# A head's output goes to one of two halves of its PSUM bank by turns, and pools are flushed where the whole plan was drained

## The chip, the cores and the metric

The kernel runs on one core of one Trainium2 chip. The metric is the device time of one execution in microseconds (us). Five engines take part: PE (TensorE, matmuls and transposes), DVE (VectorE), ACT (ScalarE), POOL (GpSimd) and SP (SyncE, which issues DMAs).

## What is computed

Causal attention with a decay bias, then a mixture layer with one dense block ("first MoE"), then one with eight experts and balanced gates ("second MoE"). In short:

```python
def _attn_ref(q, k, v, s):                      # 4 batches, 8 heads, S = 576, D = 64
    scores = (1 / sqrt(D)) * q @ k.T
    cum = cumsum(maximum(s, 0), -1)
    scores = where(causal, -1e9, scores + minimum(-(cum[:, None] - cum[None, :]), 0))
    attn = exp(scores - max(scores)); attn = attn / (sum(attn) + 1e-09)
    return attn @ v
def _moe_ref(x, w_in, w_out):                   # 2304 tokens, 512 -> 2048 -> 512
    h = x @ w_in
    return (h * sigmoid(1.702 * h)) @ w_out
def _moe2_ref(x, w_gate, w1, w2):               # 8 experts, 512 -> 1024 -> 512
    P = exp(x @ w_gate - max); 8 rounds: P by its rows' sums, then by its columns' sums
    return sum over e of P[:, e] * (maximum(x @ w1[e], 0) @ w2[e])
```

## The kernel before

**Attention.** Each of the 4 x 8 (batch, head) pairs is worked on in two parts: query blocks 0 and 1 in one unit, and query blocks 2, 3 and 4 in three units. This gives 64 "heads" n, eight in a row for each half of a batch. For a unit, `scores` makes matmuls into a score bank `sp`, from which DVE takes masked sums and their minimum (`sm`, `stats`) and ACT the exponentials; `turn` transposes them (`tp`) and copies them out (`pf`, or `ph` and `pl` from head 14 on); `values` multiplies them with V into the head's output `op`, 65 columns for each query block, whose last column is the softmax sum. When all units of a head are through, `finish` lets DVE read `op`: TENSOR_SCALAR to `stats`, RECIPROCAL, and SCALAR_TENSOR_TENSOR to `xg` (and `xgl` for the last 64 rows where there are three blocks). After eight heads, `xg` is transposed (`xtp`) and split into `xh` and `xl`, the first MoE's tokens.

**The two MoEs.** The first MoE works on blocks of 256 tokens: `mm1` makes `hp` from `xh`, `xl` and a pair of weights (`wih`, `wil`), ACT and DVE make `t`, `gh` and `gl` from it, and `mm2` adds to `acc` with `woh`, `wol`. The weights are converted on the way (`st`, `t`, casts). The last two blocks are worked on together (`wide1`, `wide2`, tile `accw`). The second MoE follows, with the banks A to D.

**What sets the order.** A planner, the class `Sequencer`, gives every operation a planned time. PE's operations are issued as they come; those of DVE, ACT, POOL and SP are held and handed out by planned time (`run`). So all traced operations have line 279, where the planner calls them, and the tiles' names tell them apart. The main loop asks functions named `can_...` for the planned time from which a step may be taken (`never` if it may not) and takes the first that is due: V's scales, the flush of `xg`, `values`, `turn`, `scores`, and only then a step of the first MoE. `settled(name, ap)` is the planned time at which all operations handed out so far on a tile, or on a part of it, are over, and infinity while one is still held; `slot` asks the same for the next buffer of a tag.

**What the change touches.** `values` takes a new `op` tile for each head from a ring of one buffer (tag "O"), which is one PSUM bank. `can_value` refuses a head that is not the next to be finished (`n > n_fin`) and asks for the slot. `first_moe` waits with `begin` until the attention and its converted weights are through, and then calls `drain`, which hands out everything that is held on all engines, before it closes the attention's pools and calls `begin_second` (which prepares the gate's scale: `gmax`, `wgs`). `flush` of a pool, which exists already, hands out only what touches the pool's tiles, with what that waits for.

Of the kernel before, what the change touches and what calls it, by code (L numbers as in the profile page):

```python
# [9 lines left out]
F32 = mybir.dt.float32  # L10
# [310 lines left out]
def kernel(  # L321
# [12 lines left out]
    seq = Sequencer()  # L334
    nc = Core(seq, tc.nc)
    seq.outside |= {x.tensor.name for x in (qk, vP, s, w_in, w_out, wg, w1, w2, out)}
    B, H, D, S = qk.shape[0], qk.shape[1], qk.shape[2] // 2, qk.shape[3] // 2
# [42 lines left out]
    apool = Pool(seq, pa.enter_context(tc.tile_pool(name="apool", bufs=2, side=right, reuse_waits="tile")))  # L380
# [452 lines left out]
    def turn(i):  # L833
# [21 lines left out]
        )  # L855
        live[i] = (ph, pl, blocks, spots)

    def values(i):
        n, u = units[i]
        qb0 = extent(n)[6][0]  # L860
        v3 = v3_of[n]
        ph, pl, blocks, spots = live.pop(i)
        if u[0] == qb0:
            outs[n] = (
                ps_a.tile([128, 3, D + 1], F32, tag="O", name="op"), stats[:, 8 + n % 2 * 3:11 + n % 2 * 3]
            )
        op, den = outs[n]
        for m, (qb, rows, ke, a) in enumerate(blocks):
            mine = [x for x in spots if x[0] == qb]
            o = op[:rows, qb - qb0, :]  # L870
            for w, (_, kb, _, at) in enumerate(mine):
                if n < N_F:
                    nc.tensor.matmul(
                        o, lhsT=ph[:, at:at + rows], rhs=v3[kb], start=(w == 0), stop=(w == len(mine) - 1)
                    )
                    continue
                for part, nv in ((ph, 2), (pl, 1)):
                    for j in range(nv):
                        v = v3[j][:, kb, :]
                        nc.tensor.matmul(  # L880
                            o[:, 0:v.shape[1]], lhsT=part[:, at:at + rows], rhs=v,
                            start=(w == 0 and part is ph and j == 0),
                            stop=(w == len(mine) - 1 and part is pl and j == nv - 1),
                        )
# [81 lines left out]
    def can_value():  # L966
        if n_v >= n_t or units[n_v][0] not in v3_of:
            return never
        n, u = units[n_v]
        if n > n_fin:  # L970
            return never
        x = [live[n_v][0], live[n_v][1], *v3_of[n]]
        return max([seq.slot(ps_a, "O") if n not in outs else 0] + [seq.settled(a.tensor.name) for a in x])

    def do_value():
        nonlocal n_v
# [918 lines left out]
    def first_moe():  # L1895

        at_pair = [0] * NB1

        def can(j):
            p = at_pair[j]  # L1900
            if p == NPAIR or 4 * p + 2 > n_conv:
                return never
            return max(
                whole(j) if at_pair[j] == 0 else 0, seq.slot(ps_m, "h"),
                seq.settled(wih[p].tensor.name), seq.settled(wil[p].tensor.name),
            )

        def second(i):
            def when():
                j, p, gh, gl = pend[0]  # L1910
                if 4 * p + 4 > n_conv:
                    return never
                t = max(seq.settled(x.tensor.name) for x in (gh, gl, woh[p], wol[p]))
                if p == 0 and i == 0:
                    t = max([t] + [
                        seq.slot(*x) for x in
                        ([(ps_a, "S1"), (ps_a, "T1")] if j == 1 else [(ps_m, "acc0"), (ps_m, "acc1")])
                    ])
                return t

            return when

        for item in range((NB1 - 2) * NPAIR):

            js = (0, 1) if item < 2 * NPAIR else (item // NPAIR,)
            yield lambda: min(can(j) for j in js)
            j = min(js, key=can)
            p = at_pair[j]
            at_pair[j] += 1
            if (j, p) == (1, 0):  # L1930
                lent[0] = True
            mm1(j, p, 0)
            yield lambda: 0
            mm1(j, p, 1)
            if at_pair[j] == NPAIR and j + 2 < NB1:
                alloc_x(j + 2)
            for i in range(2):
                if item:
                    yield second(i)
                    mm2(i)  # L1940

        def begin():
            if n_conv < len(chunks) or n_fin < len(heads) or any(pieces.values()) or vpows:
                return never
            return max(whole(j) for j in (NB1 - 2, NB1 - 1))

        for i in range(2):
            yield second(i)
            mm2(i)
        yield begin  # L1950
        seq.drain()
        pa.close()
        begin_second()
        for n in range(2 * NPAIR):
            p, i = NPAIR - 1 - n // 2, n % 2
            wide1(p, i)
            yield lambda: 0
            if n:
                wide2()
                yield lambda: 0  # L1960
            if (p, i) == (NP0 - 1, 0):
                p1b.close()
                begin_weights()
# [297 lines left out]
```

## Time and profile before

| | us |
|---|---|
| time, median of 3 runs | 1994.68 (1994.12 to 1995.38) |
| the profiled execution | 1995.91 |
| its span in the trace | 1994.1 |
| PE busy in the span | 1956.2 (98%) |
| DVE, ACT, POOL busy | 1427.6, 1227.5, 335.0 |
| PE idle in the span | 37.9 |

The profile comes from one execution, recorded by the hardware profiler. The time of an execution is a little longer than its span, which runs from the first to the last recorded instruction. An engine's busy time is a sum over stages with different limits; idle time is found by cutting the span into stretches and by reading an engine's timeline, where each idle stretch stands in square brackets with what ended it. The first part of the span, up to about 545 us, holds the attention with the first MoE's work between its steps; the wide blocks begin at about 573 us.

### The profile page before, as it was taken

How to read it: one execution, taken by the hardware profiler on the slowest of the kernel's cores; microseconds unless marked ns; L12 is line 12 of the kernel's file. 1: busy time of each engine (PE TensorE's matmuls, PEld its weight loads, DVE VectorE, ACT ScalarE, POOL GpSimd, SP SyncE). 2: the span in 40 equal slices, each digit the busy share in tenths (PEclk: the TensorE clock that was granted, in tenths of full speed). 3: DMA queues.
4: the chain of work that ended last, by engine and by line, in shares of the span. 5: the costliest groups of instructions: out<-in, count | busy, mean ns of one | idle time of the engine just before them, and what ended most of it. 6: DMA issues, size and time to landing. Idle time of an engine off the chain costs nothing.

```text
span 1994.1 us, 41095 instructions
## 1 busy us (share of the span) xinstructions
PE 1956.2 (98%) x15683; PEld 1575.5 (79%) x15683; DVE 1427.6 (72%) x3240; ACT 1227.5 (62%) x2525; POOL 335.0 (17%) x376
## 2 busy tenths in 40 slices
PE   6999999999999999999999999999999999999999
PEld 5889999999988677777777777777777777777777
DVE  5886776776743776887877767776787776776656
ACT  4776765766643665665666666656666666565343
POOL 3565444443300000000000011111100001111000
PEclk9999999999999999999999999999999999999999
DMA  7555444454335544565484565666648556566331
GB/s 221 159 178 181 138 131 138 129 146 116 86 94 186 208 152 146 202 232 182 147 273 133 153 186 156 172 197 184 167 120 261 147 150 186 156 172 183 119 130 43
DMA packets 230100, 322.11 MB, mean 162 GB/s; under 512 B 38272, under 2 KB 156224, under 8 KB 229904
## 3 DMA queue, kind: packets, MB, share of 16 engines
q1 hardware_dynamic: 216944, 295.90, 45.2%
q0 software_dynamic: 12960, 23.60, 8.2%
q8 instruction: 123, 2.02, 0.4%
q14 instruction: 73, 0.60, 0.1%
HBM read 230.85 MB, written 84.34 MB: 158 GB/s over the span
## 4 chain that ended last, share of the span: by engine, by line
PE 81%; DVE 9%; ACT 6%; DMA 2%; issue 1%; SPq 0%; POOL 0%; ACTq 0%; DVEq 0%
PE C L279 16%; PE A L279 16%; PE D L279 16%; PE hp L279 8%; PE B L279 8%; PE acc L279 5%; PE op L279 3%; PE sp L279 3%; PE tp L279 2%; ACT h L279 2%; PE accw L279 2%; DVE h L279 2%; DVE t L279 1%; DVE hst L279 1%; PE accx L279 1%
## 5 line engine op out<-in xcount | busy, mean ns | idle before, releaser
L279 PEld LDWEIGHTS <-h 128*128 128x128 f16 x6048 | 591.3, 98 | 86.3 <-issue 7.6
L279 PEld LDWEIGHTS <-w1o 128*128 128x128 f16 x4036 | 394.6, 98 | 255.1 <-issue 4.5
L279 POOL DMA_DIRECT2D acc_d<-y x90 | 77.8, 865 | 1186.5 <-DVE y L279 662.1
L279 PE MATMUL C<-xt,w1o 128*128 128x384 f16 x1152 | 218.6, 326 | 1.4 <-DVE hst L279 1.4
L279 PE MATMUL D<-xt,w1o 128*128 128x384 f16 x1152 | 218.4, 326 | 0.0
L279 PE MATMUL D<-w2o,h 128*128 128x256 f16 x1728 | 217.7, 273 | 0.2 <-ACT y L279 0.2
L279 PE MATMUL A<-xt,w1o 128*128 128x384 f16 x1152 | 214.8, 326 | 0.1
L279 PE MATMUL A<-w2o,h 128*128 128x256 f16 x1728 | 212.2, 273 | 1.7 <-ACT B L279 1.4
L279 PE MATMUL C<-w2o,h 128*128 128x256 f16 x1728 | 208.4, 273 | 2.5 <-DVE y L279 1.7
L279 DVE SCALAR_TENSOR_TENSOR h<-hst,h 128x768 f16<-128x768 f32 (+1 forms) x192 | 139.1, 755 | 55.9 <-ACT h L279 55.9
L279 ACT COPY C<-B 128x384 f32<-128x384 f32 (+1 forms) x168 | 71.5, 426 | 153.8 <-PE B L279 92.7
L279 PE MATMUL hp<-xh,wih 128*128 128x256 f32 (+1 forms) x512 | 154.4, 302 | 1.3 <-DVE t L279 0.7
L279 PE MATMUL hp<-xl,wih 128*128 128x256 f32 (+1 forms) x512 | 152.0, 297 | 0.0
L279 PE MATMUL hp<-xh,wil 128*128 128x256 f32 (+1 forms) x512 | 151.8, 297 | 0.0
L279 ACT ACTIVATE h<-hst 128x768 f16<-128x768 f32 (+1 forms) x192 | 126.2, 678 | 3.8 <-DVE hst L279 3.8
L279 ACT ACTIVATE sm<-sm,stats 64x576 f32<-64x576 f32 (+4 forms) x160 | 94.5, 600 | 34.0 <-DVE stats L279 33.7
L279 PE MATMUL acc<-gh,woh 128*128 128x256 f32 x384 | 110.9, 289 | 0.0
L279 PE MATMUL B<-w2o,h 128*128 128x256 f16 x864 | 110.5, 273 | 0.1
L279 PE MATMUL B<-xt,w1o 128*128 128x384 f16 x576 | 109.3, 326 | 0.0
L279 PE MATMUL acc<-gl,woh 128*128 128x256 f32 x384 | 108.5, 282 | 0.0
L279 PE MATMUL acc<-gh,wol 128*128 128x256 f32 x384 | 108.3, 282 | 0.0
L279 ACT COPY B<-A 128x384 f32<-128x384 f32 (+1 forms) x168 | 70.2, 425 | 58.4 <-PE A L279 57.6
(242 smaller groups left out, 4041.8 us busy)
## 6 DMA issues: line engine op xcount, KB each, us to landing
xt<-xc_d SPq DMA_DIRECT2D x168, 384.0 KB
wm<-in_moe_w_dram SPq DMA_DIRECT2D x112, 256.0 KB
w2o<-w_d SPq DMA_DIRECT2D x56, 512.0 KB
wr<-in_moe_w_dram SPq DMA_DIRECT2D x112, 256.0 KB
w_d<-wo SPq DMA_DIRECT2D x98, 256.0 KB
acc_d<-y POOLq DMA_DIRECT2D x90, 256.0 KB, 4.8
kq<-in_qk_dram SPq DMA_DIRECT2D x32, 448.0 KB
st<-in_moe_w_in_dram SPq DMA_DIRECT2D x16, 512.0 KB
```

The source lines that it names most:

```text
L279: self.seq.submit(self.name, what, lambda: method(*args, **named), outs, ins, "accum_op" in named)
```

## The change

All heads' outputs share one tile, `o_all`, of two halves of three blocks each. Head n uses half n modulo 2. `can_value` lets head n start when head n-1 is not yet finished (`n > n_fin + 1` is refused), and asks the planner for that half only. At the end of the first MoE's blocks, `drain` is replaced by a flush of the two pools that are closed next.

```diff
--- before.py
+++ after.py
@@ -855,15 +855,15 @@
         )
         live[i] = (ph, pl, blocks, spots)
 
+    o_all = ps_a.tile([128, 2, 3, D + 1], F32, name="op")
+
     def values(i):
         n, u = units[i]
         qb0 = extent(n)[6][0]
         v3 = v3_of[n]
         ph, pl, blocks, spots = live.pop(i)
         if u[0] == qb0:
-            outs[n] = (
-                ps_a.tile([128, 3, D + 1], F32, tag="O", name="op"), stats[:, 8 + n % 2 * 3:11 + n % 2 * 3]
-            )
+            outs[n] = o_all[:, n % 2], stats[:, 8 + n % 2 * 3:11 + n % 2 * 3]
         op, den = outs[n]
         for m, (qb, rows, ke, a) in enumerate(blocks):
             mine = [x for x in spots if x[0] == qb]
@@ -967,10 +967,10 @@
         if n_v >= n_t or units[n_v][0] not in v3_of:
             return never
         n, u = units[n_v]
-        if n > n_fin:
+        if n > n_fin + 1:
             return never
         x = [live[n_v][0], live[n_v][1], *v3_of[n]]
-        return max([seq.slot(ps_a, "O") if n not in outs else 0] + [seq.settled(a.tensor.name) for a in x])
+        return max([seq.settled(o_all.tensor.name, o_all[:, n % 2]) if n not in outs else 0] + [seq.settled(a.tensor.name) for a in x])
 
     def do_value():
         nonlocal n_v
@@ -1948,7 +1948,8 @@
             yield second(i)
             mm2(i)
         yield begin
-        seq.drain()
+        apool.flush()
+        ps_a.flush()
         pa.close()
         begin_second()
         for n in range(2 * NPAIR):
```

Three places of the built program follow. Names carry a buffer number; [waits X] are the engines (or DMA queues) on whose progress the instruction waits, DVE_49 being DVE's and PE_49 PE's.

PE, the second head's output at the start of the attention. Before:

```order
L279 MATMUL tp_320<-ident_60,sm_263 128x128 [waits PE_49,Activation_49]
L279 MATMUL tp_320<-ident_60,sm_263 128x128 [waits Activation_49]
L279 MATMUL tp_320<-ident_60,sm_263 128x128
L279 MATMUL sp_340<-kf_239 128x128 [waits DMAHW1_49,DMAHW0_49,DVE_49]
L279 MATMUL sp_340<-kf_239 128x256
L279 MATMUL sp_346<-kf_249 128x128 [waits DMAHW3_49,DMAHW2_49,DVE_49]
L279 MATMUL sp_346<-kf_249 128x256
L279 MATMUL op_366<-vf0_133,pf_298 128x65 [waits DVE_49,PE_49]
L279 MATMUL op_366<-vf0_133,pf_298 128x65
L279 MATMUL op_366<-vf1_134,pf_298 128x65
```

After:

```order
L279 MATMUL tp_320<-ident_60,sm_264 128x128 [waits PE_49,Activation_49]
L279 MATMUL tp_320<-ident_60,sm_264 128x128 [waits Activation_49]
L279 MATMUL tp_320<-ident_60,sm_264 128x128
L279 MATMUL op_141<-vf0_133,pf_299 128x65 [waits DVE_49]
L279 MATMUL op_141<-vf0_133,pf_299 128x65
L279 MATMUL op_141<-vf1_134,pf_299 128x65
L279 MATMUL tp_337<-ident_60,sm_284 128x128 [waits PE_49,Activation_49]
L279 MATMUL tp_337<-ident_60,sm_284 128x128 [waits Activation_49]
L279 MATMUL tp_337<-ident_60,sm_284 128x128
L279 MATMUL sp_349<-kf_240 128x128 [waits DMAHW1_49,DMAHW0_49]
L279 MATMUL sp_349<-kf_240 128x256
```

The second head's `op` (its `pf` is number 298 before, 299 after) has moved ahead of four `sp` and waits for DVE alone.

DVE ahead of the first `hp`. Before, `two1` and the rows behind it, and further on the two first `xl`:

```order
L279 TENSOR_TENSOR two1_115<-kq_359,one1_114 64x576
L279 SCALAR_TENSOR_TENSOR xg_308<-op_487,stats_124 128x2x64 [waits DVE_49]
L279 SCALAR_TENSOR_TENSOR t64_261<-st_247 128x512 [waits DMAHW4_49,Activation_49,Pool_49]
L279 TENSOR_SCALAR stats_124<-op_515 128x2 [waits PE_49]
L279 CAST wih1_76<-t64_261 128x512 [waits DVE_49]
L279 RECIPROCAL stats_124<-stats_124 128x2 [waits DVE_49]
L279 SCALAR_TENSOR_TENSOR t64_268<-st_255 128x512 [waits DMAHW3_49,Activation_49,Pool_49]
L279 SCALAR_TENSOR_TENSOR xg_308<-op_515,stats_124 128x2x64 [waits DVE_49]
L279 ISA sm_524,stats_124<-sp_525,mask_120 128x384 [waits PE_49]
```

```order
L279 TENSOR_TENSOR xl_128<-xtp_582,xh_127 128x4x128 [waits Activation_49]
L279 CAST one0_112<-kq_360 128x896 [waits DMAHW5_49,DMAHW2_49]
L279 SCALAR_TENSOR_TENSOR t64_280<-st_258 128x512 [waits DMAHW4_49,Pool_49]
L279 COPY pf_621<-tp_615 128x320 [waits DVE_49,PE_49]
L279 TENSOR_TENSOR xl_128<-xtp_601,xh_127 128x4x128 [waits Activation_49]
```

After:

```order
L279 SCALAR_TENSOR_TENSOR xg_308<-op_141,stats_124 128x2x64 [waits DVE_49]
L279 TENSOR_TENSOR two1_115<-kq_370,one1_114 64x576 [waits DMAHW7_49,Activation_49]
L279 CAST woh0_74<-t64_257 128x512 [waits DVE_49]
L279 SCALAR_TENSOR_TENSOR t64_260<-st_238 128x512 [waits DMAHW1_49,Pool_49]
L279 TENSOR_TENSOR xl_128<-xtp_504,xh_127 128x4x128 [waits Activation_49]
L279 CAST woh0_74<-t64_260 128x512 [waits DVE_49]
L279 SCALAR_TENSOR_TENSOR t64_262<-st_248 128x512 [waits DMAHW2_49,Activation_49,Pool_49]
L279 TENSOR_TENSOR xl_128<-xtp_510,xh_127 128x4x128 [waits Activation_49]
```

`xg` of the eighth head (the first row after) now stands directly ahead of `two1`, and the two `xl` follow within seven rows, with two `t64` and two `woh` casts between them; before, 24 rows lie between `two1` and the first `xl`.

PE and DVE where two heads of three blocks meet. PE before, at the start of a head's `op`:

```order
L279 MATMUL hp_788<-xh_127,wih1_76 128x256
L279 MATMUL hp_788<-xl_128,wih1_76 128x256
L279 MATMUL hp_788<-xh_127,wil1_77 128x256
L279 MATMUL op_808<-vf0_133,pf_762 128x65 [waits DVE_49,Activation_49]
L279 MATMUL op_808<-vf1_134,pf_762 128x65
L279 MATMUL op_808<-vf2_135,pf_762 128x65
```

PE after:

```order
L279 MATMUL op_141<-vf3_136,pf_775 64x65
L279 MATMUL op_141<-vf4_137,pf_775 64x65
L279 MATMUL op_141<-vf0_133,pf_786 128x65 [waits DVE_49,Activation_49]
L279 MATMUL op_141<-vf1_134,pf_786 128x65
L279 MATMUL op_141<-vf2_135,pf_786 128x65
```

DVE before, the division of such a head:

```order
L279 TENSOR_SCALAR stats_124<-op_697 128x2 [waits PE_49]
L279 TENSOR_TENSOR wil2_81<-t64_386,wih2_80 128x512 [waits Activation_49]
L279 TENSOR_SCALAR stats_124<-op_697 64x1
L279 SCALAR_TENSOR_TENSOR t64_420<-st_279 128x512 [waits DMAHW3_49,Pool_49]
L279 SCALAR_TENSOR_TENSOR t_742<-t_742,hp_670 128x512 [waits Activation_49]
L279 RECIPROCAL stats_124<-stats_124 128x3 [waits DVE_49]
L279 COPY pf_768<-tp_763 128x512 [waits PE_49]
L279 SCALAR_TENSOR_TENSOR xg_645<-op_697,stats_124 128x2x64 [waits DVE_49]
L279 SCALAR_TENSOR_TENSOR xgl_646<-op_697,stats_124 64x64
```

DVE after:

```order
L279 TENSOR_SCALAR stats_124<-op_141 128x2 [waits PE_49]
L279 TENSOR_TENSOR wil2_81<-t64_427,wih2_80 128x512 [waits Activation_49]
L279 TENSOR_SCALAR stats_124<-op_141 64x1 [waits PE_49]
L279 SCALAR_TENSOR_TENSOR t64_463<-st_280 128x512 [waits DMAHW4_49,Pool_49]
L279 RECIPROCAL stats_124<-stats_124 128x3 [waits DVE_49]
L279 ISA sm_777,stats_124<-sp_827,mask_120,stats_124 64x288 [waits PE_49]
L279 ISA stats_124 64x1
L279 SCALAR_TENSOR_TENSOR xg_669<-op_141,stats_124 128x2x64 [waits DVE_49,PE_49]
L279 SCALAR_TENSOR_TENSOR xgl_670<-op_141,stats_124 64x64
```

On PE the next head's `op` (`pf_786`) follows the last one's (`pf_775`) with nothing between them and waits for DVE, where `hp` matmuls stood ahead of it; on DVE the first `xg` now waits for PE as well as for DVE's own reciprocal.

## Rows read from the trace of the kernel before

**Rows 1.** The page's busy times (share, instructions), and the chain that ended last.

```profile
PE 1956.2 (98%) x15683; PEld 1575.5 (79%) x15683; DVE 1427.6 (72%) x3240; ACT 1227.5 (62%) x2525; POOL 335.0 (17%) x376
...
PE 81%; DVE 9%; ACT 6%; DMA 2%; issue 1%; SPq 0%; POOL 0%; ACTq 0%; DVEq 0%
```

**Rows 2.** Stretches of 100 us: length, busy us (count) by engine, PEclk, DMA share, GB/s.

```profile
0.00:100.00 100.00, 82.03 (x533) 72.14 (x533) 72.45 (x222) 61.83 (x111) 45.30 (x60) 1.00 0.62 190
100.00:200.00 100.00, 94.04 (x858) 89.65 (x858) 77.60 (x190) 70.62 (x142) 58.62 (x54) 0.97 0.56 179
200.00:300.00 100.00, 99.16 (x1014) 94.70 (x1012) 75.14 (x241) 69.64 (x147) 43.82 (x51) 1.00 0.47 135
500.00:600.00 100.00, 98.45 (x801) 89.36 (x802) 60.34 (x182) 51.02 (x105) 19.55 (x21) 1.00 0.34 96
```

**Rows 3.** PE's waits: engine tile <- releaser: us in total, times, longest us.

```profile
PE op L279 <- DVE xg L279: 6.7, 7, 2.4
...
PE op L279 <- DVE xgl L279: 1.6, 2, 0.8
```

**Rows 4.** PE's timeline, 20 to 60 us: start, us, operation, [idle before <- releaser].

```profile
20.38 1.51 PE L279 MATMUL op<-vf,pf 128*128 128x65 f32 x6
...
24.60 1.51 PE L279 MATMUL op<-vf,pf 128*128 128x65 f32 x6 [0.79 <-DVE xg L279]
...
36.24 1.51 PE L279 MATMUL op<-vf,pf 128*128 128x65 f32 x6 [1.13 <-DVE xg L279]
...
41.54 1.52 PE L279 MATMUL op<-vf,pf 128*128 128x65 f32 x6 [2.44 <-DVE xg L279]
...
49.00 0.65 PE L279 MATMUL xtp<-ident,xg 128*128 128x128 f32 x4
49.49 0.78 PE L279 MATMUL op<-vf,pf 128*128 128x65 f32 x6
...
50.39 0.40 PE L279 MATMUL sp<-two 68*128 68x512 f32 x1
...
55.30 0.36 PE L279 MATMUL hp<-xh,wih 128*128 128x256 f32 x1
```

**Rows 5.** DVE's timeline, 21 to 25 us.

```profile
21.93 0.16 DVE L279 TENSOR_SCALAR stats<-op 128x2 f32<-128x2 f32 x1 [0.68 <-PE op L279]
...
22.62 0.16 DVE L279 RECIPROCAL stats<-stats 128x2 f32<-128x2 f32 x1
23.95 0.29 DVE L279 CUSTOM_DVE_ANT_0 sm<-sp,mask 128x128 f32<-128x128 f32 x1 [1.17 <-ACT st L279]
...
24.17 0.28 DVE L279 SCALAR_TENSOR_TENSOR xg<-op,stats 128x128 f32<-128x128 f32 x1
```

**Rows 6.** PE's timeline, 9.5 to 9.9 us: the last matmuls into a score bank.

```profile
9.23 1.06 PE L279 MATMUL sp<-kf 66*128 66x256 f32 x2
```

**Rows 7.** DVE's timeline, 10 to 11 us: its first reading of that bank.

```profile
10.45 0.29 DVE L279 CUSTOM_DVE_ANT_0 sm<-sp,mask 128x128 f32<-128x128 f32 x1 [4.87 <-PE sp L279]
```

**Rows 8.** DVE's groups by shape, 5 to 570 us: busy us, mean ns, idle before.

```profile
L279 DVE SCALAR_TENSOR_TENSOR t<-st 128x512 int32<-128x512 int32 x32 | 30.0, 943 | 1.1 <-POOL wol L279 0.7 <-ACT va L279 0.3
...
L279 DVE TENSOR_TENSOR xl<-xtp,xh 128x512 fp32r<-128x512 f32 x12 | 8.2, 681 | 1.1 <-ACT xh L279 1.1
L279 DVE CAST woh<-t 128x512 fp32r<-128x512 f32 x12 | 7.8, 649 | 0.1
...
L279 DVE TENSOR_TENSOR two<-kq,one 64x576 fp32r<-64x576 f32 x1 | 1.4, 1441 | 0.0
```

**Rows 9.** PE's timeline, at 301 us and at 503 us.

```profile
301.60 0.22 PE L279 MATMUL op<-v,ph 128*128 128x65 f16 x2 [0.41 <-DVE xg L279]
...
503.57 0.22 PE L279 MATMUL op<-v,ph 128*128 128x65 f16 x2 [0.76 <-DVE xgl L279]
```

**Rows 10.** Two shorter stretches; columns as in Rows 2.

```profile
99.80:117.75 17.95, 15.44 (x167) 13.79 (x167) 13.88 (x45) 15.26 (x32) 8.94 (x10) 0.89 0.47 152
110.00:121.00 11.00, 8.49 (x67) 7.28 (x66) 9.88 (x28) 9.82 (x23) 5.93 (x8) 0.69 0.70 235
```

## The prediction

> **What bounds the kernel now.** The page's busy table comes first: PE works 98% of the span, and the chain that ended last is PE for 81% of it [rows 1]. An edit can therefore win only where PE stands idle or runs below full speed. The table by stretches says where that is: PE is busy for 82.03 us of the first 100, 94.04 of the second and 99.16 of the third, at a granted clock of 1.00, 0.97 and 1.00 [rows 2]. So some 24 us are idle in the first 200 us, under 1 us in the next 100, and 1.55 us between 500 and 600 us.
>
> The third view is PE's waits. Those of the `op` matmuls for DVE's reading of the head before (`xg`, `xgl`) are 6.7 + 1.6 = 8.3 us [rows 3]. That is the whole sum at which the first part of the change aims. PE's timeline places it: four waits early on, twice 0.79 or 0.80 (one is shown), 1.13 and 2.44, 5.16 us together [rows 4], and then single ones, of which those of 0.41 and 0.76 are shown [rows 9]. What makes the first wait long is seen on DVE: `op` of one head ends at 21.89 [rows 4], its `stats` starts at 21.93, but `xg` only at 24.17, because DVE handles its list in order and a score reading stands in front of it until 23.95 [rows 5]. 0.15 us after `xg` ends, the next head's `op` starts.
>
> **The change part by part.** In the order as built, PE's instructions are the same in number, and from about 545 us on in the same sequence. So all that can move lies in the first 545 us.
>
> *Two halves for `op`, early heads.* The planner now lets `op` of head n+1 go out before head n is divided, into the other half. But the built program still waits for all that touches the bank, whichever half it is: 54 `op` matmuls carry a wait on DVE's reads (17 before), some 45 of them on the other half, and some 31 DVE reads wait for the other head's matmuls (none before). So a wait leaves its place and comes back in another form. That the program makes bank-wide waits can be seen in this trace too: DVE's reading of the first 128 columns of a score bank starts at 10.45 [rows 7], 0.16 us after the end of the matmuls into that bank's other 256 columns, at 10.29 [rows 6].
>
> The Trainium skill ("PSUM — Partial Sum Buffer", section "PSUM bank collisions raise a hardware error") has a rule on the same side, and against this change: PSUM has to be guarded by bank and quadrant, not by address, since two engines on one bank collide at different columns as well. The row at 10.45 agrees. By the rule both halves stay one resource; without it the whole 8.3 us would be open, which is the third rival below.
>
> Of the four early waits I expect three to come back, smaller. The least that one costs is `stats` alone between two heads: 0.04 + 0.16 + 0.15 = 0.35 us; the most with nothing else on DVE is `stats`, reciprocal and `xg` in a row: 0.04 + 0.16 + 0.16 + 0.28 + 0.15 = 0.79 us, as the waits of 0.79 and 0.80 show. I take 0.72 each, so 2.2 us remain of 5.16 and 3.0 are saved.
>
> What is late next: the first MoE matmul `hp`. It now comes after 78 matmuls instead of 121, and needs `xl` of all its 256 tokens. On DVE there now stand between the last early `xg` and the second `xl` one `two`, two `t`, two `woh` casts and two `xl`: 1.44 + 2 x 0.94 + 2 x 0.65 + 2 x 0.68 = 6.0 us [rows 8], about 5.5 with each starting some 0.07 before the last one's end (23.95 + 0.29 and 24.17 show it [rows 5]). PE has eight `xtp` and four `sp` to do meanwhile: 2 x 0.65 + 4 x 0.40 = 2.9 us as at 49 to 51 us, and up to twice that at the lower speed, at which six `op` took 1.51 us instead of 0.78 [rows 4]. So 0 to 2.6 us of new idle time; I take 1.5, since at 49 us PE ran at full speed. Sum of the early phase: -3.0 + 1.5 = **-1.5 us**, between -5.2 (nothing comes back) and 0 (all comes back).
>
> *New waits on the bank after 50 us.* In the built order there are 13 places where an `op` waits for the other half's reader with at most 0.8 us of PE work since the matmuls that the reader needs; the third order piece shows one with none. Price: the rows nearest to it are the waits of 0.41 and 0.76 us [rows 9]; I take the lower, 0.4 each, since up to 0.8 us of work lies ahead of the waiting matmul. Five of the 13 lie in the stretch of the next term. The other eight cost 8 x 0.4 = 3.2, all 13 5.2 us. The waits of this kind that go with the old order are 8.3 - 5.16 = 3.1 us, of which I credit 2.3: the one of 0.76 at 503.57 has DVE late by its own work, and should stay. So +0.9 to +2.9; I take **+1.9 us**. Bounds: -2.3 (none of the 13 waits) to 13 x 0.76 - 2.3 = +7.6.
>
> *A longer run of attention only.* The order before has two stretches with 60 or more matmuls in a row and none from the MoE, of 121 and 72; after, there are three, of 169, 78 and 61. The run of 72 ends at 117.75 us. It is what such a run costs: 17.95 - 15.44 = 2.5 us idle, at a granted clock of 0.89, with ACT (15.26) and DVE (13.88) as busy as PE; and a clock of 0.69 over 11.00 us, which is 3.4 us of work lost at the lower level (1.2 of 2.4 GHz) if it is all counted [rows 10]. The clock fell while PE was idle between short `op` and `xtp` matmuls. The run of 169 has the same contents, 2.3 times as many. Ends: -3.4 if the fall of the clock does not come back, and (2.5 + 3.4) x 1.35 = +8.0 if the loss grows with the length. The middle is +2.3; I take **+2.0**, a little lower, because the longer run begins nearer to MoE work at full speed.
>
> *Flush instead of drain at 573 us.* PE's order does not change through this part. It moves the small operations for the gate's scale on DVE ahead of the first wide `t` and `gl`, and the gate weights' DMA ahead of the writes of `x_d` on SP. Behind them on DVE waits a `gl`, and for that one PE matmul group; PE's idle time between 500 and 600 us is 1.55 us in all [rows 2], with 0.76 of it at 503.57 [rows 9]. So the gain is at most 0.8, and a loss at most one 512-column operation, 0.68 [rows 8]. **0**, since DVE is busy for 60.34 of these 100 us and has room.
>
> Sum: -1.5 + 1.9 + 2.0 + 0 = **+2.4 us**. The profiled execution took 1995.91, 1.8 us of it outside the span, which nothing touches; it stood 1.23 us above the median of 1994.68. So 1998.3 by that execution, and 1994.68 + 2.4 = **1997.1 us** as a median.
>
> **The rivals.**
>
> *Slower: the long run is paced by DVE and ACT at the lower clock.* Place: the 169 matmuls ahead of 118 us. For it: the shorter run already fell to 0.69, and the new run also has five of the 13 bank waits, whose idle time is what the clock fell after. Against it: the run starts with PE at full speed. It decides from the point where the clock falls in the first half of the run. Then the third term is +8.0: -1.5 + 1.9 + 8.0 = +8.4, 2003.1 us.
>
> *Faster: the early waits go and the clock holds.* `op` of head n+1 waits only for a short `stats`, which DVE has long done; `xl` is ready in time; the fall at 110 to 121 us does not recur. That is -3.0 + 0 + 0.9 - 3.4 = -5.5, and, if early matmuls get to full speed a few us sooner (those of 1.51 against 0.78 us), a further 1 to 2 us: 1988 us. For it: PE's speed rose at about 49 us, after a row of work without a wait. Against it: DVE's list, not only PE's place in it, makes the early waits.
>
> *The change does what it says: the halves are independent.* All 8.3 us go and nothing takes their place: 1986.4 us. Against it stand the waits in the built program, and the row at 10.45.
>
> **How the numbers follow.** Within 0.2% means within about 4 us, 1990.7 to 1998.7, about what a measurement of this kernel can tell from no change. The forecast has 0.47, with its own range of 1992 to 2002: 0.37 of it within 0.2%, and 0.10 above. The slower rival has 0.25, the faster one 0.21, independent halves 0.07. Faster is 0.21 + 0.07 = 0.28, same 0.37, slower 0.10 + 0.25 = 0.35. The range runs from 1987, just under the faster rival, to 2006, which is 3 us over the slower one because its price is scaled from one shorter run; about 0.1 is left out at each end.
>
> **What would show it.** PE's idle time ahead of the early `op` matmuls (5.16 us before) should fall to about 2 us, and ahead of the first `hp` there should be 1 to 2 us of wait for `xl`. The table of PE's waits should show `op` waiting for `stats` as well as `xg`, in more and shorter waits, some 5 us after 50 us. In 60 to 120 us the granted clock should fall at least once, to about 0.7 over 10 us. From 200 us to the end the busy share should stay. If the clock row of that stretch reads 1.00 throughout, or the first `hp` starts 5 us earlier than 55.30 [rows 4] without a later run idling, the forecast is wrong on the faster side; if the clock falls at the start of the long run, on the slower side.

## The result and the profile after

The changed kernel takes **2006.45 us** (median, 2003.58 to 2007.74), the kernel before 1994.76 (1994.12 to 1995.38): a ratio of 1.0057, with an interval of 1.0039 to 1.0074. It is slower, by 11.7 us, where 2.4 us were forecast. In the experiments below, single executions of 3002, 5078 and 7422 us are left out of the ratios. Each ratio is to the kernel before as measured beside it; in the four sets of experiments its median lay between 1993.5 and 1996.1 us, so kernels of different sets are compared by their ratios.

| profiled execution | before | after |
|---|---|---|
| time, us | 1995.91 | 2007.74 |
| span | 1994.1 | 2005.9 |
| PE busy / idle in the span | 1956.2 / 37.9 | 1967.2 / 38.7 |
| start of the first wide block (`accw`) | 573.5 | 585.9 |
| at the lower clock after 52 us | 6.8 | 13.65 |

The last row is worked out from the granted clock of stretches of 5 us: a stretch of 5 us at 0.78, for example, had 2 x (1 - 0.78) x 5 = 2.2 us at the lower level. The page of after, engines and chain of waits, to be held against [rows 1]:

```profile
PE 1967.2 (98%) x15683; PEld 1580.7 (79%) x15683; DVE 1430.3 (71%) x3248; ACT 1223.8 (61%) x2515; POOL 333.6 (17%) x378
PE 79%; DVE 9%; ACT 6%; DMA 2%; issue 1%; SPq 1%; POOL 0%; ACTq 0%; DVEq 0%
```

PE has as many instructions and almost the same idle time; it was *busy* for 11 us more. The rows count a matmul as busy to its modelled end: at full clock an `hp` has 0.28 us, but the next one starts 0.12 us after it. So a successor that is a little late, and the lower clock too, add to the busy time, and the busy share alone hides the loss. By the distances between the starts of PE's rows, from 52 us to the first wide block after needs about 13 us more than before; an estimate from these rows gives 3 to 4 us of it to idle time, 3 to 4 to the lower clock and some 6 to matmuls that follow each other later at full clock. Where the loss lies is told by a landmark. The rows of the first `accw` matmuls (count: least/median/most ns, first and last start), of before and then of after:

```profile
L279 PE MATMUL accw<-gh,woh x64: 388/389/397, 573.5 to 654.8; 128*128 128x512 f32 x64
```

```profile
L279 PE MATMUL accw<-gh,woh x64: 387/389/495, 585.9 to 667.6; 128*128 128x512 f32 x64
```

12.4 us are lost by 586 us, and none behind that. The table by stretches of after (length, then busy time of PE, PEld, DVE, ACT, POOL, granted clock, DMA share, GB/s) answers to [rows 2]:

```profile
0.00:100.00 100.00, 84.70 (x529) 74.29 (x530) 62.31 (x210) 61.83 (x113) 42.99 (x58) 0.98 0.62 189
100.00:200.00 100.00, 90.72 (x819) 83.84 (x817) 81.50 (x194) 71.21 (x141) 60.65 (x60) 0.95 0.52 165
200.00:300.00 100.00, 98.25 (x955) 93.00 (x954) 67.09 (x210) 61.20 (x125) 36.03 (x42) 1.00 0.43 126
500.00:600.00 100.00, 98.60 (x868) 90.22 (x867) 64.56 (x196) 55.51 (x115) 22.63 (x24) 1.00 0.30 80
```

The second hundred has lost 3.3 us of PE's time and some clock, the third 0.9. The clock falls in three places, where before it fell in one. Stretches of 5 us of after:

```profile
75.00:80.00 5.00, 4.21 (x29) 3.66 (x28) 4.24 (x13) 3.65 (x7) 1.89 (x2) 0.88 0.78 242
80.00:85.00 5.00, 5.00 (x38) 4.71 (x38) 2.21 (x11) 3.24 (x6) 1.81 (x3) 0.78 0.50 163
110.00:115.00 5.00, 3.38 (x31) 2.94 (x32) 4.48 (x10) 2.92 (x7) 3.50 (x5) 0.79 0.34 93
115.00:120.00 5.00, 5.00 (x39) 5.00 (x39) 4.37 (x16) 2.86 (x7) 2.36 (x3) 0.86 0.13 30
180.00:185.00 5.00, 3.00 (x31) 1.81 (x27) 5.00 (x11) 3.37 (x7) 2.05 (x3) 0.96 0.71 241
185.00:190.00 5.00, 4.79 (x33) 4.57 (x34) 3.00 (x9) 3.85 (x7) 1.67 (x2) 0.50 0.29 100
190.00:195.00 5.00, 5.00 (x34) 4.57 (x34) 2.60 (x7) 3.66 (x8) 2.60 (x3) 0.86 0.60 184
```

Each fall comes in, or right behind, a stretch in which PE stood idle for 0.8 to 2 us of 5. In the last group the reader sees why PE was idle: DVE is busy for all of the 5 us. The rows of DVE and PE there (start, duration, operation, and in brackets the idle time and what ended it):

```profile
181.27 1.26 DVE L279 SCALAR_TENSOR_TENSOR t<-st 128x512 int32<-128x512 int32 x1
182.46 0.68 DVE L279 SCALAR_TENSOR_TENSOR pl<-tp,ph 128x512 f16<-128x512 f32 x1
...
183.19 0.20 PE L279 MATMUL op<-v,pl 128*128 128x65 f16 x1 [1.36 <-DVE pl L279]
```

`op` waits for `pl`, and `pl` stood on DVE behind `t`, a step of the conversion of weights for the first MoE; DVE has two of these `t` and three operations on what they made (`woh`, `wol`) between 179 and 185 us. Before, PE is busy for all of the stretch of 180 to 195 us, at a clock of 1.00:

```profile
180.00:195.00 15.00, 15.00 (x138) 14.51 (x137) 6.94 (x24) 8.58 (x15) 4.44 (x6) 1.00 0.43 144
```

PE's waits of after (us in total, times, longest):

```profile
PE op L279 <- DVE pl L279: 4.1, 6, 1.4
PE op L279 <- DVE xg L279: 2.4, 4, 1.4
PE hp L279 <- DVE xl L279: 2.0, 1, 2.0
PE op L279 <- DVE stats L279: 1.8, 5, 0.6
...
PE xtp L279 <- DVE pl L279: 1.7, 2, 1.1
PE tp L279 <- ACT sm L279: 1.7, 2, 1.0
PE sp L279 <- DVE stats L279: 1.5, 3, 0.8
```

The wait that the change aims at fell from 8.3 us [rows 3] to 2.4 + 1.8 = 4.2. What rose is waits for other readers and writers on the way of a head: `pl`, `sm`, `xl`. Before, those of `op` for `pl` were

```profile
PE op L279 <- DVE pl L279: 2.6, 4, 1.1
```

So the named waits do not add up to the loss. A second measure does: **the lag**. For a given amount of PE's matmul work (each matmul counted at the usual distance of its shape at full clock), it is the time at which a kernel has done it less the time at which before had. It is worked out from PE's rows, in us, from one profiled execution of each kernel; the columns are before's times. Its accuracy is limited: o_all_drain, told below, has after's PE order and comes to about +6 at 186 us and +10.2 at the first `accw`, so 2 us between two kernels may be a difference of executions, and at 63 us the value moves by about 1 us with the distance that is taken for each shape.

| kernel | 63 | 90 | 118 | 142 | 164 | 186 | 291 | first `accw` |
|---|---|---|---|---|---|---|---|---|
| after | -2.4 | +1.5 | +3.2 | +1.7 | +3.1 | +8.7 | +12.0 | +12.4 |
| after_free | -5.4 | -4.9 | -4.4 | -4.6 | -1.7 | +2.7 | +4.1 | +4.5 |
| new_rule_first_8 | -3.1 | -0.1 | +2.8 | +2.6 | +5.3 | +6.6 | | +7.0 |
| two_banks_first_8 | -4.7 | -0.1 | +2.0 | +2.0 | +4.3 | +5.9 | | +6.8 |
| planner_sees_bank | +0.7 | -0.4 | -0.3 | -1.9 | +5.4 | +4.3 | | +5.5 |
| conversion_first | -0.7 | -0.1 | -0.1 | +0.6 | -0.3 | +2.0 | | +5.6 |
| new_rule_from_9 | +0.8 | -0.7 | +2.5 | -0.2 | +0.2 | +0.7 | | +13.9 |

The lower rows are experiments, told below.

### The profile page after: what moved, and what is told of

Same layout as the page of the kernel before. It is cut to its first block, busy times and chain, and to the rows that moved or that the text cites. A ratio compares the mean times of both kernels' runs of the same rounds, so it can differ in the third digit from the quotient of the medians.

```text
span 2005.9 us, 41081 instructions
## 1 busy us (share of the span) xinstructions
PE 1967.2 (98%) x15683; PEld 1580.7 (79%) x15683; DVE 1430.3 (71%) x3248; ACT 1223.8 (61%) x2515; POOL 333.6 (17%) x378
## 4 chain that ended last, share of the span: by engine, by line
PE 79%; DVE 9%; ACT 6%; DMA 2%; issue 1%; SPq 1%; POOL 0%; ACTq 0%; DVEq 0%
PE C L279 16%; PE A L279 16%; PE D L279 16%; PE B L279 8%; PE hp L279 8%; PE acc L279 5%; PE op L279 3%; PE sp L279 3%; PE tp L279 2%; ACT h L279 2%; PE accw L279 2%; DVE h L279 2%; DVE hst L279 1%; DVE t L279 1%; DVE sa L279 1%
```

## The experiments

The theory after the result: the loss is made by the new order of PE's and DVE's work (the rule in `can_value`), in part through waits on the shared bank, in part through conversions of weights that come late. Rivals: the tile's layout or the flush; the bank alone; the clock alone.

**Which part of the change.** First the halves and the flush with the old rule, so that PE's instructions stand in before's order; then the new rule with the old drain.

```diff
-        if n > n_fin + 1:
+        new = False
+        if n > n_fin + (1 if new else 0):
...
-        return max([seq.settled(o_all.tensor.name, o_all[:, n % 2]) if ...
+        return max([seq.settled(o_all.tensor.name, o_all[:, n % 2] if new else None) if ...
```

> Halves and flush as in the change, but a head may still start only when the one before is divided and the whole bank is free in the plan. PE's order is then that of the kernel before on all its instructions. Theories 'order' and 'bank': 1994.8 us, within 1 us of the kernel before, since no wait for the other half is left in the way. If the tile's new place or the flush is the cause: 2000 us or more.

Measured: 1994.81 us, a ratio of 1.0004 (0.9995 to 1.0014).

```diff
-        apool.flush()
-        ps_a.flush()
+        seq.drain()
```

> The two halves alone; the drain at the end of the first MoE's blocks is kept as before. Its PE order is that of the changed kernel. Both theories put the whole loss into the first 545 us: 2006 us, within 1 us of the changed kernel. A third theory, that the flush costs several us by what it leaves on DVE ahead of the first wide block: 2003 us or less.

Measured: 2005.61 us, 1.0056 (1.0040 to 1.0072). PE's order of tiles in the traces is before's in the first kernel and after's in the second. So the layout and the flush cost and gain nothing that a measurement tells from zero, and the loss belongs to the new rule.

**Which heads.** The rule for the first eight heads alone (`new = n < 8` in the first diff), and from the ninth on (`new = n >= 8`).

> The changed kernel, but the new rule for the start of a head holds for the first 8 heads only; from the ninth on a head starts when the one before is divided and the whole bank is free. Theory 'conversion late': in the changed kernel the attention goes ahead faster from the start, the conversion of the first MoE's weights (handed out with the lowest rank) ends at 181 us instead of 163, and between 170 and 190 us PE has attention alone, with DVE full; the first heads set this off, so this kernel still ends its conversion after 172 us and takes 2000 to 2004 us. Theory 'bank': what counts is the number of waits on the other half, and these are mostly gone here: 1994 to 1998 us.

Measured: 2002.95 us, 1.0044 (1.0030 to 1.0059).

> The opposite piece: the first 8 heads by the old rule, the rest by the new one. 'Conversion late': the start is as before, the conversion ends before 170 us, 1994 to 1999 us. 'Bank': most of the waits on the other half are in this piece, 2001 to 2005 us.

Measured: 2006.66 us, 1.0067 (1.0052 to 1.0082). Each part of the rule costs by itself, and they do not add: about 9 and 13 us, by the ratios, against 11.7 for both. The second result lies nearer to the theory "bank", which had expected 2001 to 2005 us, than to that of late conversions, 1994 to 1999. The rule for the first eight heads loses by 186 us, after a gain of 3.1 us at 63; that for the other heads loses most far later, at 360 us, where the profile of new_rule_from_9 shows

```profile
360.22 0.22 PE L279 MATMUL op<-v,ph 128*128 128x65 f16 x2 [1.98 <-DVE xg L279]
```

and, in that stretch, an idle PE and a fall of the clock, where before had none (the second line is before's):

```profile
355.00:375.00 20.00, 17.66 (x170) 16.18 (x169) 13.70 (x44) 12.11 (x25) 5.20 (x7) 0.83 0.30 88
```

```profile
355.00:375.00 20.00, 20.00 (x236) 18.66 (x235) 15.39 (x48) 16.46 (x32) 9.44 (x11) 1.00 0.55 164
```

This wait is one for the bank, and in all the bank's waits of this kernel are as long as before's:

```profile
PE op L279 <- DVE xg L279: 8.6, 8, 2.4
```

The profiled execution (2009.95 us) was the slowest of four, 3.3 us above their median, so its lag is somewhat high. Still, the loss is not tied to one place of the program: the two parts of the rule lose at different places, each where the new sequence leaves PE waiting.

**What the shared bank costs.** DVE's division of a head reads a constant tile (`ident`) instead of `op`, while the planner still believes that it reads `op`. PE's and DVE's order stays, and no division waits for the bank or holds it.

```diff
-                out=den[:r, c0:c1], in0=op[:r, c0:c1, D], ...
+                    out=den[:r, c0:c1], in0=ident[:r, 0:c1 - c0], ...
-                in0=op[:r, c0:c1, 0:D], ...
+                    in0=ident[:r, 0:(c1 - c0) * D].rearrange("p (a d) -> p a d", a=c1 - c0), ...
```

> The changed kernel in its own order, but DVE's division of a head reads a constant tile in SBUF in place of the output bank, so that no matmul and no division waits for that bank (the attention's result is therefore not the reference's). Theory 'order': the 11.7 us come from the new order, in which PE stands idle for reads of other tiles (pl, sm, xl, xtp) and its clock falls more often; this kernel then stays at 2000 to 2004 us, and 8 us or more above the same edit of the kernel before. Theory 'bank': the waits on the other half of the bank are the loss, with the clock falls that follow them; this kernel then comes to 1993 us or less, and to no more than the same edit of the kernel before.

Measured: 2001.36 us, 1.0038 (1.0024 to 1.0051).

> The kernel before in its own order with the same edit (the division reads a constant tile, so the attention's result is not the reference's). Its op matmuls waited 8.3 us for the division. Both theories: faster than before by at most those 8.3 us and by what the clock gives back, 1986 to 1993 us; if DVE's other work is late at the same places, nearer to 1993. What tells the theories apart is the distance to the other kernel of this kind: 'order' 8 to 12 us, 'bank' 0 us or below.

Measured: 1997.68 us, 1.0016 (1.0006 to 1.0025). That is *slower* than before by 3.3 us, where both theories had expected it to be faster, and the distance of the two edited kernels is 3.7 us, between the 8 to 12 of the theory "order" and the 0 of the theory "bank". In after's order the edit is worth 2005.61 - 2001.36 = 4.3 us against o_all_drain beside it, and 5.1 against after itself.

These are not clean prices of the waits, for the edit also made DVE's division longer. The operation that writes most of `xg` (mean ns after the busy time), before and in before_free:

```profile
L279 DVE SCALAR_TENSOR_TENSOR xg<-op,vpow,stats 128x128 f32<-128x128 f32 x50 | 17.2, 344 | 12.4 <-PE xtp L279 12.0
```

```profile
L218 DVE SCALAR_TENSOR_TENSOR xg<-ident,vpow,stats 128x128 f32<-128x128 f32 x50 | 29.1, 583 | 12.6 <-PE xtp L280 12.2
```

In all DVE is busy for 1454.4 us in before_free against 1427.6 in before, and for 1450.0 in after_free against 1430.3 in after. For the heads behind the eighth, no run takes the waits away without this. If the edit by itself costs after's order the 3.3 us that before lost by it, the bank's share would be 7.5 us instead of 4.3; that is an estimate, and the share of the order alone would then be the 3.7. In after_free, `op` and `tp` wait longer for `pl` and `sm` than in after, which fits a later DVE:

```profile
PE op L280 <- DVE pl L280: 5.0, 6, 1.6
PE tp L280 <- ACT sm L280: 2.8, 4, 0.9
```

The lag says when: without the bank the new order is 5.4 us ahead at 63 us and still 4.6 at 142; with it, 2.4 ahead and then 1.7 behind. From 142 to 186 us both lose about the same, 7.3 and 7.0 us (o_all_drain some 5). So that second loss is there without any wait for the bank, though the longer division may have a part in after_free's.

A real second bank for the odd ones of the first eight heads (a tile of `ps_m`, which is not in use yet) points the same way. PE's and DVE's order is that of new_rule_first_8:

```diff
-    o_all = ps_a.tile([128, 2, 3, D + 1], F32, name="op")
+    def op_bank(n):
+        return (ps_m, "acc1") if n < 8 and n % 2 else (ps_a, "O")
...
```

> The first 8 heads' outputs go by turns to two whole banks (the second is one that the first MoE needs only from about 61 us on); from the ninth head on the old rule and one bank. The order is that of the kernel with the new rule for the first 8 heads (2002.95 us); only the waits on the other half are gone. 'Bank' for these heads: the stretch up to 60 us ends 5 us earlier than in the kernel before (in the changed kernel with no bank waits at all it was 5.4), and the time comes to 1996 to 1999 us. 'Conversion late': the gain is there at 60 us and mostly gone again at 190 us, where the conversion is late as before; 2000 to 2003 us.

Measured: 1999.37 us, 1.0029 (1.0017 to 1.0040). By the ratios that is 3.0 us better than with one bank, but the two intervals overlap. The early gain is 4.7 us instead of 3.1, and 9 us are lost between 63 and 164 us all the same. The profiled execution (2002.56 us) was the slowest of seven, so its lag shows the loss as larger than the median has it.

Then the planner was told the truth: its `where` gives the whole bank for an `op` tile, so that it plans with the waits that the program has.

```diff
+        if ap.space == PSUM and ap.tensor.name.startswith("op"):
+            return (0, 128), (0, 2048)
```

> The changed kernel, but the planner takes every access to the output tile as one to the whole bank, as the built program's waits do; a head may still start before the one before is divided, if the plan then allows it. Its longest attention-only runs are those of the kernel before (121 and 72 matmuls). Both theories expect most of the loss to go, 1993 to 1998 us: 'bank', because no wait is left out of the plan; 'conversion late', because the heads no longer run ahead (the conversion then ends before 170 us).

Measured: 2000.95 us, 1.0036 (1.0024 to 1.0049). Between a third and a half of the loss goes (4 us by the ratios, 5.5 by the medians); both theories had expected 1993 to 1998 us. The rest stands at one place. The stretch of planner_sees_bank, and the wait in it:

```profile
150.00:170.00 20.00, 16.26 (x127) 14.96 (x126) 16.05 (x38) 14.77 (x29) 9.90 (x9) 0.91 0.61 198
```

```profile
161.96 0.38 PE L281 MATMUL hp<-xh,wih 128*128 128x256 f32 x1 [1.60 <-DVE t L281]
```

This `t` is made from the last `hp`, and it was late by ACT's part of it, not by a conversion on DVE, which stood idle ahead of it:

```profile
161.22 0.69 DVE L281 SCALAR_TENSOR_TENSOR t<-t,hp 128x512 f32<-128x512 f32 x1 [1.08 <-ACT t L281]
```

Before, the same stretch is

```profile
150.00:170.00 20.00, 18.55 (x164) 17.85 (x164) 16.82 (x35) 14.85 (x30) 10.72 (x10) 1.00 0.56 177
```

**Whether late conversions are the cause.** The 32 steps `t<-st` start, before and after, between

```profile
L279 DVE SCALAR_TENSOR_TENSOR t<-st x32: 670/692/1796, 22.0 to 163.1; 128x512 int32<-128x512 int32 x32
```

```profile
L279 DVE SCALAR_TENSOR_TENSOR t<-st x32: 672/725/1761, 28.2 to 181.3; 128x512 int32<-128x512 int32 x32
```

so the last one is 18 us late. They have rank 2 in the planner, behind the attention. An edit gives conversions 8 to 15 rank 1:

```diff
-        seq.rank = 2
+        seq.rank = 1 if 8 <= c < 16 else 2
```

> The changed kernel with one number changed: the weights' conversions 8 to 15 are handed out with rank 1 instead of 2, so that they don't stand behind all of the attention's work on DVE, ACT and POOL. 'Conversion late': the stretch without MoE matmuls at 170 to 190 us and the fall of the clock in it go away, 5 to 7 us faster than the changed kernel, 1999 to 2002 us. 'Bank': nothing of that kind, 2004 to 2008 us.

Measured: 2001.82 us, 1.0040 (1.0025 to 1.0055). The last `t<-st` now starts at 166.6 us, and the place at which after lost most is full:

```profile
180.00:195.00 15.00, 15.00 (x138) 14.47 (x137) 7.73 (x24) 7.46 (x15) 5.00 (x5) 1.00 0.55 179
```

With the conversions out of that place, its hole is gone, as the theory of late conversions had expected. But that was 3.4 us by the ratios and 4.6 by the medians, of 11.7, and planner_sees_bank, whose last conversion starts at 163.3 (before: 163.1), still loses 7 us between 142 and 164 us. Late conversions are one form of the loss, not its common cause.

Four kernels joined the second bank with this rank, for conversions 8 to 15, 9 to 13, 6 to 13 and 4 to 15, to see if both cures together reach before.

> The same with the weights' conversions 8 to 15 handed out with rank 1. 'Conversion late': keeps part of the early gain, 1994 to 1999 us, and less than the same kernel without it by 3 us or more. 'Bank': as without it, within 2 us. If this is the version that the change aimed at, it is faster than the kernel before: below 1992.

Measured: 2009.21 us, 1.0072 (1.0050 to 1.0093).

> Two whole banks for the first 8 heads, conversions 9 to 13 (the ones that were late) with rank 1. 'Conversion late': the thirteenth conversion starts before 85 us instead of 94, the lag of 6 us at 190 us goes, and some of the 4.7 us won by 58 us stays: 1990 to 1996 us. 'Any other order costs': the early gain is gone by 90 us, and PE's short waits and clock falls come back elsewhere: 1997 to 2005 us. Longest attention-only run 136 matmuls; if that length set the time, between the kernels with 105 (2001.8) and 162 (1999 to 2003).

Measured: 2004.46 us, 1.0051 (1.0033 to 1.0070).

> The same with conversions 6 to 13. Longest attention-only run 102. 'Conversion late': 1990 to 1996 us. 'Any other order costs': 1997 to 2005 us. 'Run length': below the kernel with 136.

Measured: 2001.31 us, 1.0028 (1.0015 to 1.0041).

> The same with conversions 4 to 15. Longest attention-only runs 116 and 72. 'Conversion late': 1990 to 1996 us, unless the conversions now hold up the attention, which shows as a lag already at 60 us. 'Any other order costs': 1997 to 2005 us. 'Run length': between the two others.

Measured: 2003.09 us, 1.0042 (1.0029 to 1.0055). The two cures do not add; the first of the four has the highest median of all kernels. Its stretch of 110 to 125 us shows what it bought:

```profile
110.00:125.00 15.00, 9.74 (x94) 7.73 (x93) 12.09 (x39) 10.75 (x24) 8.12 (x9) 0.75 0.62 207
```

PE is idle for 5.3 us of 15. Counted in the traces, the longest row of matmuls without MoE work behind the first `hp` is 131 here and 179 in after (169 in the prediction's count of the built program). So the length of that row, on which the prediction's third term was scaled, does not order the kernels: with 72, as before, planner_sees_bank takes 2000.95 us, and with 175 two_banks_first_8 takes 1999.37.

**Whether the clock of the first 49 us matters.** Before, with 14 matmuls of 512 columns put ahead of its own work.

> The kernel before with 14 matmuls of 512 columns on a constant tile put in front, while PE has nothing to do until 8.7 us (their result is overwritten). It measures the price of the lower clock of the first 49 us by itself: PE is busy there for 33 us. If the clock is then at its upper level from the first score matmul on and stays: 6 to 14 us of PE time less up to 49 us, of which DVE's and the DMAs' waits eat half, 1986 to 1991 us. If it falls back at the first pauses: 1993 to 1996 us, and the rows show at which.

Measured: 1994.70 us, 1.0001 (0.9991 to 1.0011). The extra matmuls raise the clock at 6.6 us, and it falls back at 16.9 us, in the first long wait of the kernel's own work; the wait, and the stretches around it:

```profile
17.40 2.90 PE L279 MATMUL sp<-kf 66*128 66x128 f32 x8 [3.44 <-DMA kf<-in_qk_dram]
```

```profile
8.60:16.90 8.30, 4.96 (x31) 3.90 (x31) 6.36 (x25) 5.99 (x14) 0.00 (x0) 1.00 0.90 230
16.90:51.00 34.10, 26.65 (x104) 22.35 (x105) 21.37 (x77) 15.26 (x30) 12.00 (x10) 0.50 0.69 232
```

Nothing is left of it at 63 us, where the lag is +0.8: a higher clock in the first 17 us bought no time behind them.

**All sixteen kernels.** Ten of them: the start of the first `accw`, beside the time at the lower clock and PE's idle time, both from 52 us to that start:

| kernel | first `accw` | lower clock | idle |
|---|---|---|---|
| halves_old_rule | 572.0 | 0 | 11.9 |
| before | 573.5 | 6.8 | 11.7 |
| after_free | 578.0 | 6.8 | 14.7 |
| planner_sees_bank | 579.0 | 10.2 | 13.0 |
| two_banks_first_8 | 580.3 | 10.2 | 16.3 |
| new_rule_first_8 | 580.5 | 10.2 | 14.9 |
| o_all_drain | 583.7 | 10.2 | 15.5 |
| after | 585.9 | 13.7 | 15.2 |
| two_banks_conversion | 587.1 | 20.5 | 19.4 |
| new_rule_from_9 | 587.4 | 17.1 | 17.9 |

Over all sixteen the start goes with either column (correlation 0.81 and 0.85). That they go together is no proof of which comes first; in each stretch shown above the idle time stands ahead of the fall or in the same 5 us. The clock alone does not make the time: of before's executions in the set of after_free, the three with a mean granted clock of 1.000 took 1994.5 to 1996.3 us, and the eleven with 0.998, as in the profiled one, 1992.7 to 1995.6. So before's one fall costs nothing that can be measured. In two_banks_first_8 the execution at 1.000 took 1996.36 us and the one at 0.995 2002.55; there they go together, and which makes which is not shown.

**What is settled, and what stays open.** Settled: layout and flush are worth nothing; the new rule makes the loss; its largest piece in after lies between 142 and 186 us, where conversions crowd DVE and PE runs out of MoE work. Shown in part: the waits on the one bank have a share, 4 to 5 us as measured with after_free, whose longer division may make that too low. Open: how the loss divides between the bank and the order, and which property of an order avoids such holes. Each of the nine other PE orders lost 5 to 14 us by the first `accw`, at places of its own, and neither the conversions' time nor the length of the attention-only rows foretold which. No kernel here beats before by more than a measurement can tell.

## Why the prediction was wrong

- **Where it can move: right.** All of the loss lies ahead of 586 us.
- **Early heads: mechanism right, and the size nearly.** Forecast -1.5 us, measured -2.4 at 63 us, with an uncertainty of about 1 us. The `xl` wait ahead of the `hp` came, 2.03 us against 1.5 forecast:

```profile
33.05 1.54 PE L279 MATMUL op<-vf,pf 128*128 128x65 f32 x6 [0.20 <-DVE xg L279]
...
39.96 1.33 PE L279 MATMUL xtp<-ident,xg 128*128 128x128 f32 x5 [1.40 <-DVE xg L279]
...
42.74 0.58 PE L279 MATMUL hp<-xh,wih 128*128 128x256 f32 x1
45.35 0.58 PE L279 MATMUL hp<-xl,wih 128*128 128x256 f32 x1 [2.03 <-DVE xl L279]
...
45.94 0.41 PE L279 MATMUL hp<-xh,wih 128*128 128x256 f32 x1
46.16 0.41 PE L279 MATMUL hp<-xl,wih 128*128 128x256 f32 x1
```

  The `op` waits for a division that are left over are well under the 2.2 us that were kept, one of 0.20 us; a wait for `xg` of 1.40 us stands ahead of `xtp` instead. What the sum did not have: the first `hp` is 12.6 us earlier than 55.30 [rows 4] and so runs at the lower clock, 0.21 us from one to the next instead of 0.12 later. Without any bank wait (after_free) the early phase gains 4.4 to 5.4 us, next to the bound of 5.2 that the prediction gave for it.
- **The new bank waits: the right term, probably too small.** Forecast +1.9 (bounds -2.3 to +7.6), measured 4 to 5 with after_free, with part of that in the early phase and with the reserve told there. The step counted 13 places at 0.4 us each, by the rows of 0.41 and 0.76 [rows 9], and 2.3 us of old waits as a credit. But the named waits of `op` fell, from 8.3 to 4.2 us, and the loss was still there; so the rows named `op` don't show where it is paid. The rule on PSUM banks that the prediction quoted (the Trainium skill, "PSUM — Partial Sum Buffer", section "PSUM bank collisions raise a hardware error") points the right way: the halves are not independent, and both after_free and two_banks_first_8 gain when nothing has to wait for the one bank. The rival of independent halves, at 1986.4 us, falls by the waits; and after_free, which comes nearest to that case, still takes 2001.36.
- **The longer run: its cost is not what its length says.** Forecast +2.0, at 60 to 121 us. Measured between 63 and 142 us +4.1 in after, but only +0.8 in after_free, in the same order; by this most of it is the bank again. The long row stands at 94.65 to 115.35 us, and the clock fell at its end, at 113 us, as before [rows 10]; the fall at 79 us belongs to a shorter row ahead of it. Both last for about as long in sum as before's one. So the slower rival had the right sign and came within 3.3 us (2003.1), by luck: its condition, a fall in the first half of the long row, did not come.
- **Missing: 142 to 186 us. This is the step that failed.** The prediction's sum has no term there, which puts it at nothing without a reason; measured were +7 us in after and after_free, and some 5 in o_all_drain. By the lag, after's 12.4 us are -2.4 up to 63 us, +4.1 up to 142 (forecast, both terms together, +3.9), +7.0 up to 186 and +3.7 behind. The prediction looked for runs of 60 or more matmuls without the MoE; the one here has 56 in the trace, at 179 to 187 us, and lay under the line that was drawn. For this term it also looked only at what PE does in a row, not at what DVE does beside it: the conversions that the new order puts off until 181 us.
- **"From 200 us the busy share stays": not quite.** 98.25 against 99.16 us of the third hundred, and 3.3 us of lag between 186 and 291 us.
- **Flush instead of drain: right**: 0 us, as nearly as two kernels 0.8 us apart can show (2005.61 and 2006.45).

Of the signs it named, three came: the `xl` wait, `op` waiting for `stats` (1.8 us in five waits), and a fall of the clock in 60 to 120 us, though as two short ones and not as 0.7 over 10 us. The range's upper end, 2006, lay just under the median, because each bound was taken inside the stretches that the prediction had looked at.

## What to carry to other kernels

When a scheduler's rule is loosened, the operation that may now start early can be the smallest part of the change. Here what was pushed behind it on the other engines (the conversion of weights, and with it the MoE matmuls that fill PE's gaps) weighed more, and was paid some 100 us later. Compare the orders of *all* engines over the whole region, without a cut-off on what counts as a long run, and give a reordering of a schedule that is 98% full a loss of several us as its own case. A planner that thinks two halves of a PSUM bank are independent, where the program waits for the whole bank, plans with times that the run does not keep; telling it so gave back between a third and a half of the loss. And an edit that takes a wait away to price it has to be checked for what else it changes: here it made the division longer.

## What the runs showed of the hardware that was not expected

- The clock's falls are not a fixed property of an order. Before and halves_old_rule have the same PE order; before fell to the lower level for 6.8 us at 114 us, with PE idle for 2.5 of these 15 us, and halves_old_rule, with PE idle for 4 us of the same 15, did not fall (before, then halves_old_rule):

```profile
110.00:125.00 15.00, 12.49 (x101) 11.28 (x100) 13.56 (x35) 12.28 (x28) 8.51 (x9) 0.77 0.76 245
```

```profile
110.00:125.00 15.00, 11.05 (x103) 9.37 (x102) 14.13 (x35) 12.28 (x28) 9.37 (x9) 1.00 0.77 248
```

  Their first `accw` start 1.5 us apart (572.0 and 573.5).
- Up to about 49 us of before, and 51 of after, the clock column reads 1.00, though the matmuls run at half speed (in after 0.21 us from one `hp` to the next at 46 us, later 0.12). Only the spacing of equal matmuls shows the level there; in warm_start, which had been at the upper level first, the same column reads 0.50.
- DVE's division took longer when it read a constant tile in place of the output bank, though the shapes are the same: 583 ns against 344 on average for the largest group of `xg`, while the median row of that group has 352; a few rows take up to 1550. What lengthens these is not shown.
